# The input sums of a Winograd MLP spread over a chunk's third and fourth double pair, and the first row of a spectrum made one item for both batches

## The chip, the core and the metric

The kernel runs on one core of a Trainium2 chip. The core has five engines with an instruction queue each: TensorE (PE, with its weight loads shown apart as PEld), VectorE (DVE), ScalarE (ACT), GpSimd (POOL) and SyncE (SP), which here issues nearly all DMAs. An engine takes its instructions in order; between engines they wait for each other through semaphores. The metric is the device time of one execution in microseconds, lower is better.

## What is computed

Three stages follow each other on x of shape (2, 3008, 256), all in float32: a real FFT along the sequence with a complex linear layer, a soft threshold of 0.01 and the inverse FFT; a SiLU MLP (256 to 2048 to 256); a leaky-ReLU MLP of the same size.

```python
X = np.fft.rfft(x, axis=1)
Yr = Xr @ w_r - Xi @ w_i + b_r
Yi = Xr @ w_i + Xi @ w_r + b_i
Yr = np.sign(Yr) * np.maximum(np.abs(Yr) - lam, 0.0)
...
y = np.fft.irfft(Y, n=x.shape[1], axis=1)
...
h = x @ w_in
g = h * (1.0 / (1.0 + np.exp(-h)))
return (g @ w_out).astype(np.float32)
...
g = np.maximum(0.01 * h, h)
```

## The kernel before

Every float32 product is made of three matmuls: each operand is split into a high part (`hi`, a cast) and a low part (`lo`, the operand minus `hi`), and lo x hi, hi x lo and hi x hi are added up in PSUM.

The order of instructions is written out by hand (`manual_schedule`): the program's order is each engine's order.

**The spectrum.** 3008 is 47 x 64. A first DFT over 47 (`pa`, line 284) leaves rows k = 0 to 23 for each of two batches. An *item* (k, b) is one row of one batch; the list `items` has 48. The function `spectrum(j)` runs a pipeline over items: `mix` (matmuls `pz`, the complex linear layer), `split_z` (cast `zh`, subtraction `zl`), `seed` (the bias is copied into the PSUM tile `py`), `forward` (six `py` matmuls with the table `dm` of that k), `threshold`, `split_y`, `backward` (three `pb` matmuls), `store` (a DMA to a buffer `scr` in DRAM). `load_dm` and `split_dm` bring and split the tables ahead of time. Row k = 0 is real and has one column for each batch: `mix` runs once for both, then item (0, 0) uses rows 0 to 63 of the result and of the table and item (0, 1) uses rows 64 to 127, each with its own `forward` on 64 rows, `backward` and `store`.

Between the items, `fifth_w` runs a fifth of a step of the decoding of the first MLP's weights: the raw tile `wraw` is loaded by SyncE and made into `wc` and `wm` by ScalarE first (lines 142 and 144). The tiles `pz` have two buffers in PSUM.

**The inverse** (`inverse`, line 444) reads `scr` back as `bt`, 96 rows of which two are zero.

**The MLPs** work through 12 chunks of 512 tokens (the last of 384) in each layer, and in each chunk through eight pairs of 128 hidden units. In chunks 2 to 10 of the second layer (`FAST`) pairs go two at a time, as a *double pair*; `both_pairs` writes out the order of one, and a chunk has four, with p = 0, 2, 4 and 6. In it `pr` is the even pair, whose first layer is made plainly (`first`), and `fa` the odd pair, whose first layer is made with Winograd's seven products (`unit`, line 619): products 1 and 2, later 6 and 7, then 5 and 4, then 3. Product 7 begins anew in the PSUM tile that product 2 had filled, so it waits until `join` on VectorE (line 627, `f<-ph,kept`) has read it; `join` also reads the copy `kept` that ScalarE makes. `one` and `two` are the pairs of the double pair before, whose second layer (`products`, line 690) is made here. For `one`, VectorE's first operation in a double pair is `low("1")` (`l<-f,h`).

Products 5, 6 and 7 and 4 read sums of the chunk's input blocks, which are made one chunk ahead. `ahead` gives the steps of this as a list: load the input (`load_x2`), split it (`split_x2`), make four sums (`sums_x2`: t1 and t3 on GpSimd, then t2 and t4 on VectorE, where t2 reads t1), split the sums (`split_xs`: two casts on ScalarE, one subtraction on VectorE, one on GpSimd). `make_next` takes one step from the list: in the middle of a double pair (after `pr.low("1")`), but at its end (after `fa.t1()`) where p is 4. So a chunk's four double pairs hold load, split, sums, split of the sums, one each. For chunk 2 the steps stand in the ordinary pairs of chunk 1.

Of the kernel before, what the change touches and what calls it, by code (L numbers as in the profile page):

```python
# [9 lines left out]
F32 = mybir.dt.float32  # L10
# [3 lines left out]
ALU = mybir.AluOpType  # L14
# [25 lines left out]
def dft_tables():  # L40
# [13 lines left out]
    for k in range(KH):  # L54
# [16 lines left out]
        dm[k, 0, :, 4], dm[k, 1, :, 4] = wt * s, wt * sg * c  # L71
    dm[0, 1, :, :3] = dm[0, 0, :, :3]

    dm[..., 3:, :] = dm[..., 3:, :].reshape(KH, 2, R2, 2, R2 // 2, 2).swapaxes(-1, -2).reshape(KH, 2, R2, 2, R2)
    as32 = lambda a, *sh: np.ascontiguousarray(a.reshape(sh).astype(np.float32))
    da = np.concatenate([da[:80], np.zeros((NP - NM, 128)), da[80:]])
    return as32(da, NP, 128), as32(ea, NJ, PAIR), as32(dm, KH, 128, 320)


@with_exitstack  # L80
def spectral_mlp_kernel(ctx, tc, x, w_r, w_i, b_r, b_i, w_in1, w_out1, w_in2, w_out2, da, ea, dm, out):
# [13 lines left out]

    scr = dram.tile([KH * 4, B, R2 // 2, D], F32, name="scr")
    scr2 = dram.tile([128, 2, TOK], F32, name="scr2")
    ea_sb = const.tile([NJ, PAIR], F32, name="ea_sb")

# [127 lines left out]
    bias = fft.tile([128, D], F32, name="bias")  # L227
    items = [(k, b) for k in range(KT) for b in range(B)] + [(k, b) for b in range(B) for k in range(KT, KH)]
    dm_raw, dm_t, z_p, z_t, y_p, y_t, b_p = ({} for _ in range(7))

    def new_dm(j):
        return j < len(items) and (items[j][0] >= KT or items[j][1] == 0)

    def load_dm(j):
# [17 lines left out]
    with tc.tile_pool(name="xp", bufs=6) as xp:  # L252
# [27 lines left out]
        for c in range(R2 // NA):  # L280
# [19 lines left out]
            if c == 10:  # L300
                for g, w in enumerate((w_r, w_i)):
                    nc.sync.dma_start(out=wms[g], in_=w.rearrange("(h p) e -> p h e", p=128))
            elif c == 11:
                load_dm(0)
                for g, w in enumerate((b_r, b_i)):
                    nc.sync.dma_start(out=bias[g * 64:(g + 1) * 64, :], in_=w.rearrange("(o e) -> o e", o=1).to_broadcast([64, D]))
                load_dm(2)
            elif c == 12:
                nc.sync.dma_start(out=ea_sb, in_=ea)
            elif c == 13:  # L310
                for g in range(2):
                    nc.scalar.copy(wm["hi"][:, :, g], wms[g])
                    nc.gpsimd.tensor_tensor(out=wm["lo"][:, :, g], in0=wms[g], in1=wm["hi"][:, :, g].bitcast(F32), op=ALU.subtract)
# [7 lines left out]
    def mix(j):  # L321
        k, b = items[j]
        if j == 1:
            return
        r = B * (B * (k - 1) + b + 1) if k else 0
# [10 lines left out]
    def split_z(j):  # L336
        if j == 1:
            z_t[1] = z_t[0]
            return
        pz = z_p.pop(j)  # L340
        hi = f3.tile([128, 2, D], F32R, tag="zh", name="zh")
        lo = f3.tile([128, 2, D], F32R, tag="zl", name="zl")
        src = pz.rearrange("p (g e) -> p g e", g=2)
        nc.scalar.copy(hi, src)
        nc.vector.tensor_tensor(out=lo, in0=src, in1=hi.bitcast(F32), op=ALU.subtract)
        z_t[j] = hi, lo

    def seed(j):
        if j in y_p:
            return  # L350
        y_p[j] = ps_h.tile([128, 512], F32, tag="h", name="py")[:, :D]
# [63 lines left out]
    seed(1)  # L415
    spectrum(-1)
    n_items = len(items)
    for j in range(n_items):
# [53 lines left out]

    def sums_x2(c):
        b = [quarter(x2f[c][h], k) for h in range(2) for k in range(2)]
        t = xsum[c] = [stage.tile([128, 512], F32, tag="wraw", name="xsum", bufs=2) for _ in range(2)]
        t1, t2, t3, t4 = (quarter(u, k) for u in t for k in range(2))
        for d, x, y, eng in ((t1, b[1], b[0], nc.gpsimd), (t3, b[3], b[1], nc.gpsimd),
                             (t2, b[3], t1, nc.vector), (t4, b[2], t2, nc.vector)):
            eng.tensor_tensor(out=d, in0=x, in1=y, op=ALU.subtract)  # L479
        xs[c] = homes[c % 2].tile([128, 2, 1024], F32R, tag="hold0", name="xs")  # L480

# [299 lines left out]
    def both_pairs(i):  # L781
# [170 lines left out]
```

## Time and profile before

| | |
|---|---|
| median of 3 runs | 1161.02 us (1160.89 to 1161.34) |
| the profiled execution | 1160.99 us, span 1159.0 us |
| TensorE busy | 1141.4 us, 98% of the span |
| VectorE busy | 867.5 us, 75% |
| ScalarE busy | 816.7 us, 70% |
| GpSimd busy | 668.5 us, 58% |
| granted TensorE clock | 1.0 throughout |

The span runs from the first to the last instruction; 2 us of the execution's time lie outside it. A matmul's end is modelled, so what a matmul costs in a dense stretch is read from the distance of the starts. The chain that ended last runs over TensorE for 82% of the span. The list `todo` is what moves work between engines in the second layer, and the waits there are read in one double pair of one chunk and hold for the others.

### The profile page before, as it was taken

The page shows a single profiled execution, that of the slowest core. Times are in us where ns is not written, and L with a number is a line of the kernel's source. Part 1 is how long each engine was busy: PE and PEld are TensorE (multiplying, and loading weights), DVE is VectorE, ACT ScalarE, POOL GpSimd, SP SyncE. Part 2 cuts the span into 40 slices and gives each one's busy share as a digit, 9 for nine tenths or more (in the row PEclk, how much of TensorE's full clock was granted, in tenths as well). Part 3 has the DMA queues.
Part 4 walks back from the last instruction along what each step waited for, and adds up shares of the span by engine and source line. Part 5 has one row for each costly group of instructions (what it writes and reads, how often), then busy time and mean ns, then how long its engine had stood idle before and what let it go on. Part 6 is the DMA issues. An engine that isn't in the chain of part 4 may idle for free.

```text
span 1159.0 us, 21096 instructions
## 1 busy us (share of the span) xinstructions
PE 1141.4 (98%) x7608; PEld 1052.2 (91%) x7608; DVE 867.5 (75%) x1484; ACT 816.7 (70%) x1720; POOL 668.5 (58%) x683
## 2 busy tenths in 40 slices
PE   9999999999999999999999999999999999999998
PEld 9888888889999999999999999989899889988998
DVE  4898956455666666676674778899999999999973
ACT  4788876666676676666666777777777777777774
POOL 0567836444444444454453777767677677667652
PEclk9999999999999999999999999999999999999999
DMA  9445543010111210111110111010000100101000
GB/s 243 120 135 158 167 120 93 20 51 19 57 54 38 68 60 29 51 60 35 38 37 1 37 32 37 20 37 20 26 30 20 37 20 20 37 20 33 20 6 27
DMA packets 36184, 61.80 MB, mean 53 GB/s; under 512 B 3952, under 2 KB 16080, under 8 KB 36080
## 3 DMA queue, kind: packets, MB, share of 16 engines
q1 hardware_dynamic: 35792, 60.28, 17.4%
q8 instruction: 60, 0.98, 0.4%
q14 instruction: 44, 0.36, 0.1%
q10 hardware_dynamic: 288, 0.18, 0.1%
HBM read 41.83 MB, written 18.61 MB: 52 GB/s over the span
## 4 chain that ended last, share of the span: by engine, by line
PE 82%; DVE 9%; issue 4%; POOL 2%; ACT 2%; DMA 0%; SPq 0%; ACTq 0%; POOLq 0%
PE acc L690 33%; PE ph L582 31%; PE pz L332 6%; PE ph L619 4%; PE py L361 3%; PE px L444 2%; PE pa L284 2%; DVE u L664 2%; DVE l L645 2%; PE pb L384 1%; DVE f L627 1%; POOL u L657 1%; DVE lb L645 1%; POOL la L645 1%; DVE xsum L479 1%
## 5 line engine op out<-in xcount | busy, mean ns | idle before, releaser
L645 POOL TENSOR_TENSOR la<-u,ha 128x512 fp32r<-128x512 f32 (+1 forms) x176 | 245.4, 1395 | 199.7 <-ACT ha L683 195.2
L645 DVE TENSOR_TENSOR lb<-u,hb 128x768 fp32r<-128x768 f32 (+1 forms) x176 | 193.7, 1100 | 154.6 <-ACT hb L683 154.0
L582 PE MATMUL ph<-xhi,winhi 128*128 128x512 f32 (+1 forms) x624 | 188.1, 382 | 0.0
L582 PE MATMUL ph<-xlo,winhi 128*128 128x512 f32 (+1 forms) x624 | 188.0, 381 | 0.0
L582 PE MATMUL ph<-xhi,winlo 128*128 128x512 f32 (+1 forms) x624 | 187.2, 380 | 0.1
L657 POOL TENSOR_TENSOR u<-u 128x256 f32<-128x256 f32 x160 | 150.9, 943 | 32.0 <-ACT u L597 22.2
L683 ACT CAST hb<-u 128x768 fp32r<-128x768 f32 (+1 forms) x176 | 141.2, 802 | 33.5 <-DVE u L671 31.5
L690 PE MATMUL acc<-hb,wlo 128*128 128x256 f32 (+1 forms) x496 | 137.8, 278 | 0.0
L690 PE MATMUL acc<-lb,whi 128*128 128x256 f32 (+1 forms) x496 | 137.5, 277 | 0.0
L690 PE MATMUL acc<-hb,whi 128*128 128x256 f32 (+1 forms) x496 | 137.5, 277 | 0.0
L582 PEld LDWEIGHTS ph<-xhi,winhi 128*128 128x128 f32 x624 | 116.4, 187 | 21.7
L582 PEld LDWEIGHTS ph<-xlo,winhi 128*128 128x128 f32 x624 | 116.4, 187 | 21.3 <-POOL xlo L467 0.3
L582 PEld LDWEIGHTS ph<-xhi,winlo 128*128 128x128 f32 x624 | 104.4, 187 | 9.6 <-ACT u L599 0.2
L683 ACT CAST ha<-u 128x512 fp32r<-128x512 f32 (+1 forms) x176 | 109.1, 620 | 3.6 <-PE acc L690 1.9
L597 ACT ACTIVATE ph<-ph 128x512 f32<-128x512 f32 (+1 forms) x112 | 64.7, 578 | 63.8 <-PE ph L582 63.8
L690 PE MATMUL acc<-ha,wlo 128*128 128x256 f32 (+1 forms) x352 | 99.1, 282 | 0.0
L690 PE MATMUL acc<-ha,whi 128*128 128x256 f32 (+1 forms) x352 | 98.8, 281 | 0.0
L690 PE MATMUL acc<-la,whi 128*128 128x256 f32 (+1 forms) x352 | 98.8, 281 | 0.0
L690 PE MATMUL acc<-h,wlo 128*128 128x256 f32 (+1 forms) x336 | 94.7, 282 | 0.0
L597 ACT ACTIVATE u<-ph 128x512 f32<-128x512 f32 (+1 forms) x80 | 47.1, 588 | 67.1 <-PE ph L582 65.2
L690 PE MATMUL acc<-l,whi 128*128 128x256 f32 (+1 forms) x336 | 93.6, 278 | 0.0
L690 PE MATMUL acc<-h,whi 128*128 128x256 f32 (+1 forms) x336 | 93.5, 278 | 0.0
(157 smaller groups left out, 3099.8 us busy)
## 6 DMA issues: line engine op xcount, KB each, us to landing
wraw<-in_moe_w_in_dram SPq DMA_DIRECT2D x32, 256.0 KB
wraw<-in_moe_w_out_dram SPq DMA_DIRECT2D x32, 256.0 KB
scr<-bo SPq DMA_DIRECT2D x48, 128.0 KB
scr<-x2o SPq DMA_DIRECT2D x22, 256.0 KB
x2i<-scr SPq DMA_DIRECT2D x22, 256.0 KB
out_dram<-x2o SPq DMA_DIRECT2D x22, 256.0 KB
dmr<-in_dm_dram SPq DMA_DIRECT2D x34, 160.0 KB
bt<-scr SPq DMA_DIRECT2D x14, 384.0 KB
```

Of the source, the lines that this page charges most:

```text
L284: nc.tensor.matmul(pa[h][:, s * 128:(s + 1) * 128], lhsT=xt[c][:, s, h * 128:(h + 1) * 128], rhs=da_sb, start=True, stop=True, skip_group_ ...
L332: nc.tensor.matmul(turned(pz), lhsT=u[:, h, :], rhs=turned(v[:, h].rearrange("p g e -> p (g e)")), start=(n == 0), stop=(n == len(terms) - 1))
L361: nc.tensor.matmul(turned(py), lhsT=u, rhs=turned(v), start=False, stop=(n == len(terms) - 1), skip_group_check=True)
L444: nc.tensor.matmul(px[:, s * PAIR:(s + 1) * PAIR], lhsT=bt[:, s, h * 128:(h + 1) * 128], rhs=ea_sb, start=True, stop=True, skip_group_chec ...
L582: nc.tensor.matmul(turned(ph), lhsT=u[:, h, f % HALF * 128:][:, :128], rhs=turned(v[:, h, :]), start=(i == 0), stop=(i == len(terms) - 1))
L597: nc.scalar.activation(out=out, in_=ph, func=ACTF.Silu)
L619: nc.tensor.matmul(turned(self.ph[dst]), lhsT=u, rhs=turned(m), start=(begin and i == 0), stop=(i == 2), skip_group_check=True)
L645: eng.tensor_tensor(out=lo, in0=src, in1=hi.bitcast(F32), op=ALU.subtract)
L657: nc.gpsimd.tensor_tensor(out=blk(1), in0=blk(0), in1=blk(2), op=ALU.subtract)
L664: nc.vector.tensor_tensor(out=v[:, 3:5], in0=b22, in1=v[:, 0:2], op=ALU.subtract)
L683: nc.scalar.copy(hi, src)
L690: nc.tensor.matmul(turned(dst), lhsT=u, rhs=turned(v), start=(begin and self.p == 0 and i == 0), stop=(end and self.p == NF // 2 - 1 and i ...
```

## The change

There are two parts.

*The sums.* `sums_x2` is split in two steps: the first makes t1 and t3 on GpSimd, the second t2 and t4 on VectorE. `make_next` is called in the middle of the fourth double pair as before and now also at its end (`pr.p >= 4`). So the four double pairs hold load; split; GpSimd's sums (at the end); VectorE's sums (in the middle) and the split of the sums (at the end).

*Row k = 0.* The items become 47: (0, 0) stands for both batches. Its table is built anew so that one `forward` on 128 rows makes the real and imaginary parts of both batches; it needs a second table (`dm[KH]`, 128 of its columns, called "rest" here) for the second matmul of each kind, which is loaded and split ahead (`load_rest`, `split_rest`). Its bias tile `bias0` (printed as `bias_103` or `bias0_103`) is filled by two broadcasts, and two single rows of it are then written again with `b_r`. It is stored by two DMAs of half the size. Two zero rows go from `scr`, `ea` and `bt` (94 for 96).

```diff
-    dm[0, 1, :, :3] = dm[0, 0, :, :3]
-
...
+    dm = np.concatenate([dm.reshape(KH, 128, 320), np.zeros((1, 128, 320))])
+    dm[0] = 0
...
+        u0, u1, back = dm[0, :, 64:192], dm[KH, :, :128], dm[0, :, 192:]
+        u0[n, q], u1[n, q] = c[:, :-1], s[:, :-1]
...
-    items = [(k, b) for k in range(KT) for b in range(B)] + [(k, b) for b in range(B) for k in range(KT, KH)]
+    bias0 = fft.tile([128, D], F32, name="bias0")
+    items = [(0, 0)] + [(k, b) for k in range(1, KT) for b in range(B)] + [(k, b) for b in range(B) for k in range(KT, KH)]
...
+    def split_rest():
+        hi, lo = (dmp.tile([128, 320], F32R, tag=q, name=q, bufs=7)[:, :128] for q in ("dmh", "dml"))
+        raw = dm_raw.pop("rest")[:, :128]
+        nc.scalar.copy(hi, raw)
+        nc.gpsimd.tensor_tensor(out=lo, in0=raw, in1=hi.bitcast(F32), op=ALU.subtract)
+        dm_t["rest"] = hi, lo
...
-                load_dm(2)
+                load_rest()
+                load_dm(1)
+                for r0, r1, w in ((0, 64, b_r), (64, 128, b_i)):
+                    nc.sync.dma_start(out=bias0[r0:r1, :], in_=w.rearrange("(o e) -> o e", o=1).to_broadcast([64, D]))
+                for r0 in (64, 96):
+                    nc.sync.dma_start(out=bias0[r0:r0 + 1, :], in_=b_r.rearrange("(o e) -> o e", o=1))
...
-        if j == 1:
-            return
...
-        nc.vector.tensor_copy(y_p[j], bias)
+        nc.vector.tensor_copy(y_p[j], bias if j else bias0)
...
-        rows = slice(j * 64, j * 64 + 64) if j < 2 else slice(0, 128)
-        terms = [(u[rows, 64 * (1 - g):64 * (3 - g)], v[rows, g, :]) for u, v in ((dl, zh), (dh, zl), (dh, zh)) for g in range(2)]
+        tables = [[u[:, 64 * (1 - g):64 * (3 - g)] for g in range(2)] for u in (dh, dl)]
+        if j == 0:
+            for t, u in zip(tables, dm_t.pop("rest")):
+                t[1] = u
+        dh, dl = tables
+        terms = [(u[g], v[:, g, :]) for u, v in ((dl, zh), (dh, zl), (dh, zh)) for g in range(2)]
...
-        nc.sync.dma_start(out=scr[4 * k:4 * k + 4, b], in_=bo)
+        if k:
+            nc.sync.dma_start(out=scr[4 * k - 2:4 * k + 2, b], in_=bo)
+        else:
+            for b in range(B):
+                nc.sync.dma_start(out=scr[0:2, b], in_=bo[b * R2:(b + 1) * R2, :])
...
+    split_rest()
...
-        fifth_w(j % 5 if j < 2 * KT else (j - 2 * KT) % 3)
+        fifth_w(j % 5 if j < 2 * KT - 1 else (j - 2 * KT + 1) % 3)
...
-    def sums_x2(c):
+    def sums_x2(c, late_ones):
...
+        for d, x, y in ((t2, b[3], t1), (t4, b[2], t2)) if late_ones else ((t1, b[1], b[0]), (t3, b[3], b[1])):
+            (nc.vector if late_ones else nc.gpsimd).tensor_tensor(out=d, in0=x, in1=y, op=ALU.subtract)
...
-                    lambda: sums_x2(c), lambda: [split_xs(c, k, e) for k, e in engines]]
+                    lambda: sums_x2(c, False), lambda: sums_x2(c, True), lambda: [split_xs(c, k, e) for k, e in engines]]
...
-        if pr.p == 4:
+        if pr.p >= 4:
```

On VectorE, before, from the end of a third double pair to the first `join` of the next chunk (the first and last `lb` here end a double pair):

```order
L645 TENSOR_TENSOR lb<-u,hb 128x768
L479 TENSOR_TENSOR xsum<-x2i,xsum 128x256 x2
L645 TENSOR_TENSOR l_9682<-f_9602,h_9681 128x512
L627 TENSOR_TENSOR f_9735<-ph,kept 128x256
...
L645 TENSOR_TENSOR lb<-u,hb 128x768
L645 TENSOR_TENSOR l_9730<-ph,h_9729 128x512
L485 TENSOR_TENSOR xs<-xsum,xs 128x512
L645 TENSOR_TENSOR lb<-u,hb 128x768
L645 TENSOR_TENSOR l_9819<-f_9735,h_9818 128x512
L627 TENSOR_TENSOR f_9865<-ph,kept 128x256
```

The same engine in the change, from the first `join` of the fourth double pair to the first `join` of the next chunk:

```order
L663 TENSOR_TENSOR f_9723<-ph,kept 128x256
...
L681 TENSOR_TENSOR lb<-u,hb 128x768
L681 TENSOR_TENSOR l_9718<-ph,h_9717 128x512
L516 TENSOR_TENSOR xsum<-x2i,xsum 128x256 x2
L681 TENSOR_TENSOR lb<-u,hb 128x768
L521 TENSOR_TENSOR xs<-xsum,xs 128x512
L681 TENSOR_TENSOR l_9805<-f_9723,h_9804 128x512
L663 TENSOR_TENSOR f_9855<-ph,kept 128x256
```

The sums moved from ahead of the fourth double pair's first `join` to behind its `l<-ph,h`, and `xs` moved from there to behind the second `lb`; three operations instead of one stand between that `l` and the next chunk's first `join`.

On SyncE in the change, at the start of the spectrum, with the semaphores that each DMA waits for (`dmr_347` is the rest table, `dmr_349` the table of k = 1, lanes DMAHW0 to 7 count landings):

```order
L337 DMA bias0_103<-in_b_r_dram 64x256 [waits DMAHW2_49]
L337 DMA bias0_103<-in_b_i_dram 64x256 [waits DMAHW3_49]
L339 DMA bias0_103<-in_b_r_dram 1x256 [waits DMAHW4_49,DMAHW3_49]
L339 DMA bias0_103<-in_b_r_dram 1x256 [waits DMAHW5_49]
L341 DMA ea_sb_76<-in_ea_dram 94x94 [waits DMAHW6_49]
L150 DMA wraw_402<-in_moe_w_in_dram 128x512 [waits DMAHW7_49]
```

The four DMAs of `bias0` are new and stand ahead of `ea_sb` and the first `wraw`; the third waits on the lane of the second (DMAHW3).

On ScalarE in the change, at the same place:

```order
L273 CAST dmh<-dmr 128x320
L257 CAST dmh<-dmr 128x128
L157 ACTIVATE wc<-wraw 128x256
L159 ACTIVATE wm<-wraw 128x256
L371 CAST zh<-pz 128x512 x2
```

The cast of the rest table is new; `wc` and `wm` of the first `wraw` stand ahead of the first `zh`, as before.

## Rows read from the trace of the kernel before

**Rows 1.** The page, part 1: engine, busy us (share), instructions.

```profile
PE 1141.4 (98%) x7608; PEld 1052.2 (91%) x7608; DVE 867.5 (75%) x1484; ACT 816.7 (70%) x1720; POOL 668.5 (58%) x683
```

**Rows 2.** Waits of TensorE: waiter, releaser, us in total, times, longest.

```profile
PE ph L619 <- DVE f L627: 12.7, 8, 1.6
```

**Rows 3.** Timeline of TensorE: start, length, line, out<-in, count, idle before; chunk 5.

```profile
871.50 0.85 PE L619 MATMUL ph<-xs,ws 128*128 128x256 f32 x6
...
901.48 0.50 PE L619 MATMUL ph<-xs,ws 128*128 128x256 f32 x3
903.57 0.63 PE L619 MATMUL ph<-xs,ws 128*128 128x256 f32 x3 [1.58 <-DVE f L627]
```

**Rows 4.** Timeline of VectorE, third to fourth double pair of chunk 5 and on.

```profile
899.68 1.81 DVE L479 TENSOR_TENSOR xsum<-x2i,xsum 128x256 f32<-128x256 f32 x2 [1.33 <-POOL xsum L479]
901.42 1.75 DVE L645 TENSOR_TENSOR l<-f,h 128x512 fp32r<-128x512 f32 x1
...
908.16 1.18 DVE L485 TENSOR_TENSOR xs<-xsum,xs 128x512 fp32r<-128x512 f32 x1
909.26 2.04 DVE L645 TENSOR_TENSOR lb<-u,hb 128x768 fp32r<-128x768 f32 x1
```

**Rows 5.** Timeline of VectorE, first double pair of chunk 5.

```profile
869.41 1.22 DVE L645 TENSOR_TENSOR l<-f,h 128x512 fp32r<-128x512 f32 x1
870.56 0.41 DVE L627 TENSOR_TENSOR f<-ph,kept 128x256 f32<-128x256 f32 x1
...
875.72 0.68 DVE L645 TENSOR_TENSOR l<-ph,h 128x512 fp32r<-128x512 f32 x1
876.33 1.45 DVE L645 TENSOR_TENSOR lb<-u,hb 128x768 fp32r<-128x768 f32 x1
```

**Rows 6.** Timeline of GpSimd, first and fourth double pair of chunk 5.

```profile
875.57 1.39 POOL L645 TENSOR_TENSOR la<-u,ha 128x512 fp32r<-128x512 f32 x1 [2.63 <-ACT ha L683]
...
898.91 1.44 POOL L479 TENSOR_TENSOR xsum<-x2i 128x256 f32<-128x256 f32 x2
...
901.18 1.45 POOL L645 TENSOR_TENSOR la<-u,ha 128x512 fp32r<-128x512 f32 x1
```

**Rows 7.** Timeline of ScalarE, fourth double pair of chunk 5.

```profile
900.17 0.36 ACT L624 COPY kept<-ph 128x256 f32<-128x256 f32 x1
```

**Rows 8.** Timeline of TensorE, start of the spectrum and one later period.

```profile
36.57 0.61 PE L332 MATMUL pz<-wmhi,ahi 128*128 128x512 f32 x2
...
40.97 0.38 PE L332 MATMUL pz<-wmhi,alo 128*128 128x512 f32 x1
...
97.44 0.62 PE L332 MATMUL pz<-wmlo,ahi 128*128 128x512 f32 x2
...
98.80 0.39 PE L361 MATMUL py<-zh,dml 128*128 128x256 f32 x2
...
99.82 0.62 PE L332 MATMUL pz<-wmlo,ahi 128*128 128x512 f32 x2
```

**Rows 9.** Timeline of SyncE's DMA issues, start of the spectrum.

```profile
26.00 0.58 SPq L306 DMA_DIRECT2D bias<-in_b_r_dram  x1
27.15 0.49 SPq L306 DMA_DIRECT2D bias<-in_b_i_dram  x1
...
28.94 1.88 SPq L135 DMA_DIRECT2D wraw<-in_moe_w_in_dram  x2
...
35.42 0.33 SPq L237 DMA_DIRECT2D dmr<-in_dm_dram  x1
```

**Rows 10.** Timelines of ScalarE and VectorE, start of the spectrum.

```profile
34.33 0.45 ACT L142 ACTIVATE wc<-wraw 128x256 uint32<-128x256 uint32 x1
...
35.88 0.58 ACT L344 CAST zh<-pz 128x512 fp32r<-128x512 f32 x1 [0.74 <-PE pz L332]
...
36.50 0.69 DVE L345 TENSOR_TENSOR zl<-pz,zh 128x512 fp32r<-128x512 f32 x1 [0.54 <-ACT zh L344]
```

**Rows 11.** Windows: stretch, length, busy us (instructions), clock, DMA share, GB/s.

```profile
36.00:37.30 1.30, 1.30 (x7) 0.85 (x6) 0.80 (x2) 0.54 (x2) 0.75 (x1) 1.00 0.47 126
```

More of the change, by code (lines that the diff above doesn't have):

```diff
@@ L71, in dft_tables @@
         dm[k, 0, :, 4], dm[k, 1, :, 4] = wt * s, wt * sg * c
-    dm[0, 1, :, :3] = dm[0, 0, :, :3]
     dm[..., 3:, :] = dm[..., 3:, :].reshape(KH, 2, R2, 2, R2 // 2, 2).swapaxes(-1, -2).reshape(KH, 2, R2, 2, R2)
+    dm = np.concatenate([dm.reshape(KH, 128, 320), np.zeros((1, 128, 320))])
+    dm[0] = 0
+    th = 2 * np.pi * ((R1 * np.arange(R2 // 2 + 1)[:, None] * n2[None, :]) % S) / S
+    c, s = np.cos(th).T, np.sin(th).T
+    s[:, -1] = 0
+    half = R2 // 2
+    for b in range(B):
+        n, q = slice(b * R2, (b + 1) * R2), slice(b * half, (b + 1) * half)
+        im = slice(R2 + b * half, R2 + (b + 1) * half)
+        u0, u1, back = dm[0, :, 64:192], dm[KH, :, :128], dm[0, :, 192:]
+        u0[n, q], u1[n, q] = c[:, :-1], s[:, :-1]
+        u0[n, im], u1[n, im] = -s[:, :-1], c[:, :-1]
+        u0[n, im.start], u1[n, im.start] = c[:, -1], s[:, -1]
+        order = lambda a: a.reshape(-1, half, 2).swapaxes(-1, -2).reshape(-1, R2)
+        back[q, n] = order(c[:, :-1].T * np.where(np.arange(half) == 0, 1.0, 2.0)[:, None] / S)
+        back[im, n] = order(-2 * s[:, :-1].T / S)
+        back[im.start, n] = order(c[:, -1:].T / S)[0]
     as32 = lambda a, *sh: np.ascontiguousarray(a.reshape(sh).astype(np.float32))
     da = np.concatenate([da[:80], np.zeros((NP - NM, 128)), da[80:]])
-    return as32(da, NP, 128), as32(ea, NJ, PAIR), as32(dm, KH, 128, 320)
+    return as32(da, NP, 128), as32(np.delete(ea.reshape(NJ, PAIR), (2, 3), 0), NR, PAIR), as32(dm, KH + 1, 128, 320)
 @with_exitstack
@@ L94, in spectral_mlp_kernel @@
     stage = pool("stage", 3)
-    scr = dram.tile([KH * 4, B, R2 // 2, D], F32, name="scr")
+    scr = dram.tile([NR, B, R2 // 2, D], F32, name="scr")
     scr2 = dram.tile([128, 2, TOK], F32, name="scr2")
-    ea_sb = const.tile([NJ, PAIR], F32, name="ea_sb")
+    ea_sb = const.tile([NR, PAIR], F32, name="ea_sb")
     parts = ("hi", "lo")
@@ L232, in new_dm, with load_rest @@
         return j < len(items) and (items[j][0] >= KT or items[j][1] == 0)
+    def load_rest():
+        dm_raw["rest"] = dmp.tile([128, 320], F32, tag="dmr", name="dmr", bufs=3)
+        nc.sync.dma_start(out=dm_raw["rest"], in_=dm[KH])
+    def split_rest():
[4 more added lines that the diff above has]
+        dm_t["rest"] = hi, lo
     def load_dm(j):
@@ L336, in split_z @@
     def split_z(j):
-        if j == 1:
-            z_t[1] = z_t[0]
-            return
         pz = z_p.pop(j)
@@ L390, in store @@
         nc.scalar.copy(bo, b_p.pop(j))
-        nc.sync.dma_start(out=scr[4 * k:4 * k + 4, b], in_=bo)
+        if k:
+            nc.sync.dma_start(out=scr[4 * k - 2:4 * k + 2, b], in_=bo)
+        else:
+            for b in range(B):
+                nc.sync.dma_start(out=scr[0:2, b], in_=bo[b * R2:(b + 1) * R2, :])
     STAGES = [(split_z, 1), (threshold, 3), (split_y, 4), (seed, 1), (store, 6), (mix, 0), (forward, 2), (backward, 5)]
@@ L409, in load_b @@
             b, p = divmod(g, R2 // 2)
-            bt = btp.tile([NJ, NG, D], F32, tag="bt", name="bt")
+            bt = btp.tile([NR, NG, D], F32, tag="bt", name="bt")
             nc.sync.dma_start(out=bt[:, :n], in_=scr[:, b, p:p + n, :])
@@ L471, in spectral_mlp_kernel @@
     quarter = lambda a, k: a[:, k * 256:(k + 1) * 256]
-    def sums_x2(c):
+    def sums_x2(c, late_ones):
         b = [quarter(x2f[c][h], k) for h in range(2) for k in range(2)]
[L475 to L480, printed above, removed]
+        if not late_ones:
+            xsum[c] = [stage.tile([128, 512], F32, tag="wraw", name="xsum", bufs=2) for _ in range(2)]
+            xs[c] = homes[c % 2].tile([128, 2, 1024], F32R, tag="hold0", name="xs")
+        t1, t2, t3, t4 = (quarter(u, k) for u in xsum[c] for k in range(2))
+        for d, x, y in ((t2, b[3], t1), (t4, b[2], t2)) if late_ones else ((t1, b[1], b[0]), (t3, b[3], b[1])):
+            (nc.vector if late_ones else nc.gpsimd).tensor_tensor(out=d, in0=x, in1=y, op=ALU.subtract)
     def split_xs(c, k, eng):
```

## The prediction, made before the change was timed

> **What bounds the kernel now.** The page was read first, then the waits of TensorE, then the stretches where it waits, engine by engine. TensorE (PE) is busy for 98% of the span [rows 1], so a change can win only by removing its matmuls or its waits. The waits view names one wait of weight: the matmuls of `unit` (line 619) stand 8 times, 1.6 us at the longest, for VectorE's `join` (line 627) [rows 2]. Its other lines are small and lie at the start of the program.
>
> Rows 3 show one of the eight, in chunk 5 of the second MLP layer. The three matmuls of product 6 start at 901.48; a 256-column matmul takes a slot of 0.114 us (1.02 for nine [rows 8]), so product 7 is due at 901.82, and it starts at 903.57. The true cost is thus 1.75 us (the view counts 1.58, from the modelled end of the matmul before). In the chunk's first double pair the same six matmuls run without a gap [rows 3]: product 7 is there at 871.50 + 0.35 = 871.85. Eight waits (chunks 2 to 9, which prepare chunks 3 to 10) cost 8 x 1.75 = 14.0 us.
>
> Why VectorE is late [rows 4]: it stands from 898.35 for 1.33 us in front of its two input sums (`xsum`), since their first operand comes from GpSimd, whose own two `xsum` start at 898.91 [rows 6]. The sums take 1.81, then `l<-f,h` takes 1.75 (it runs beside GpSimd's `la`, 901.18 to 902.63 [rows 6]), and `join` comes behind it; product 7 starts when it is done. ScalarE is not the cause: its `kept` copy, the other input of `join`, ends at 900.53 [rows 7].
>
> **Part 1, the sums and their splits.** GpSimd's two sums stay at the end of the third double pair. VectorE's two go to the middle of the fourth, ahead of its second `lb`; the split of the sums (two ScalarE casts, one subtraction on VectorE, one on GpSimd) goes from there to the end of the fourth. Nothing is added: one chunk has the same instructions.
>
> Gain at the old place: VectorE's `l<-f,h` can follow `lb` at about 898.6, and `join` then waits only for `kept`, as it does in the first double pair (870.56, just behind `l<-f,h` [rows 5]). So `join` ends near 901.0, before 901.82, and the 1.75 us are gone there.
>
> What is late next is the same queue one double pair on. The fourth double pair now runs as the first does, 901.82 - 871.85 = 29.97, call it 30.0 us later. VectorE's `l<-ph,h` ended at 876.40 there [rows 5], so it ends at 906.40 here. Behind it stand the two sums, `lb`, the split `xs`, `l<-f,h` and the next chunk's first `join`; product 7 of that chunk is due one double pair (10.0 us) after 901.82, at 911.8. The pieces, each from its nearest row: the sums 0.82 (two 256-column operations at the 0.41 of a `join` [rows 5]) to 1.81 [rows 4]; `lb` 1.45 [rows 5] to 2.04 [rows 4]; `xs` 1.18 [rows 4] to 1.75, the longest 512-column operation [rows 4]; `l<-f,h` 1.22 [rows 5] to 1.75 [rows 4]; `join` 0.41. Five starts overlap the end before them by 0.08 each (876.33 against 876.40), 0.4 in all.
> Low ends: 0.82 + 1.45 + 1.18 + 1.22 + 0.41 - 0.4 = 4.7, so 911.1: no wait. High ends: 1.81 + 2.04 + 1.75 + 1.75 + 0.41 - 0.4 = 7.4, so 913.8: a wait of 2.0.
> Taken: sums 1.81, since GpSimd's `la` of the fourth double pair stands beside them until about 906.96 (875.57 + 1.39 + 30.0 [rows 6]) and its `u` next; `lb` 1.65, between its ends, since GpSimd's half of the split can start only behind the second ScalarE cast; `xs` 1.18, `l<-f,h` 1.22. Sum 5.9, so 912.3: a new wait of 0.5 us at the next chunk's first double pair. Each chunk gains 1.75 - 0.5 = 1.25, eight gain **10.0 us** (bounds: 14.0 gained to 2.0 lost).
>
> VectorE operations with one operand in PSUM (`l<-ph,h`) show 0.68 beside `la`; those with two operands in SBUF stretch: `l<-f,h`, which begins 0.24 after `la`, ends at 903.17, that is 0.54 after `la` [rows 4, 6]. The Trainium skill (SBUF — State Buffer, "Who interferes with whom") says that a VectorE instruction with two SBUF inputs and a GpSimd instruction that reads SBUF exclude each other, the second one blocked until the first is over; the row agrees. By that rule every moved operation could be held for a whole GpSimd instruction, which is the second rival below.
>
> Who else sees the moved work: ScalarE's two casts now precede the cast `h<-f` that `l<-f,h` reads. The second cast waits for the second sum (908.1 by the terms above); two casts behind that, at about 0.6 each as `zh` [rows 10], end near 909.4, and `l<-f,h` is reached only at 910.7. So ScalarE costs nothing here as long as VectorE's queue covers it; without that cover `join` would come up to 0.6 earlier than ScalarE allows, inside the bounds. TensorE reads the split sums first in products 6 and 7, so these come no later than `join` itself. No DMA moves.
>
> The first preparation (for chunk 2) lies in ordinary pairs; its split moves from the seventh to the eighth pair, right ahead of chunk 2's first `join`. No row prices it; its bounds are nothing and one `xs` (1.18). Taken: **0.5 us lost**, once.
>
> **Part 2, row k = 0 as one item.** Batch 1's item goes: six `py` and three `pb` matmuls of 256 columns. In a steady period these take 99.82 - 98.80 = 1.02 us and the six `pz` matmuls 98.80 - 97.44 = 1.36 [rows 8], on the path, since TensorE bounds this stage too: **1.02 gained**. The two k = 0 items were also the only matmuls on 64 rows. From 36.57 to 40.97 [rows 8] TensorE did five pairs of `pz` matmuls (five thirds of 1.36, or 2.27) and two `py` groups (two thirds of 1.02 each, or 1.36): 3.63 of 4.40 us, so about 0.76 are gaps. **0.76 gained** if they go with the 64-row matmuls.
> The Trainium skill (TensorEngine Tiling (Array Packing), "Key Properties") says that a change of tiling mode drains TensorE. By it all of the 0.76 goes; the rows alone only place the gaps between the two kinds of matmul, and would leave the gain of this item anywhere between nothing and all of it.
>
> What it adds, at the start: one table load in place of a later one, two more broadcasts for `bias0`, and two single-row DMAs that overwrite part of the second broadcast, so SyncE waits for that to land before it issues them (the order after shows the wait). `ea_sb` and the first `wraw` loads are queued behind them. ScalarE needs the first `wraw` for `wc` and `wm`, which stand ahead of the first `zh` in its order. Before, `wraw` was issued at 28.94 [rows 9] and had long landed when `wc` ran at 34.33 [rows 10]. After: the two `bias` broadcasts took 1.64 (26.00 to 27.64 [rows 9]); with the rest table, table 1 and `bias0` the second broadcast is issued at about 30.2. A table load that met an idle queue was issued at 35.42 [rows 9] and moved its bytes between 36.0 and 37.3 [rows 11], so a landing comes at least 1.9 after the issue: 32.1, or 33.0 behind the backlog. Then two rows, `ea_sb` and `wraw` at 0.4 each: `wraw` issued at 33.3 to 34.2, landed 1.9 to 3.0 later, at 35.2 to 37.2. From `wc` to the end of the first `zl` it takes 0.45 twice (`wc`, and `wm` of the same size), 0.58 and 0.69, less the overlaps about 2.1 [rows 10], and the third `pz` group needs the buffer that this `zl` frees. TensorE is ready for it at 37.05. With `wraw` at 36.5, TensorE waits until 38.7: **1.7 lost**; bounds 0.3 and 2.3.
> The rest (one item fewer per engine, 94 for 96 rows in the inverse, one weight step fewer in the loop) lies beside TensorE, which shows no wait from there to the second layer [rows 2]. Part 2 sums to -1.02 - 0.76 + 1.7, about **0.1 gained**.
>
> **The sum.** Against the profiled execution (1160.99, 0.03 from the median of the runs): 1160.99 - 10.0 + 0.5 - 0.1 = **1151.4 us**.
>
> **The rivals.** (1) The wait does not come back: the low ends hold, each chunk gains 1.75: 1160.99 - 14.0 + 0.3 - 0.1 = 1147.2. For it: the sums no longer start right behind two GpSimd instructions. Against: three operations instead of one stand in the next `join`'s queue. (2) GpSimd gets in first and holds most of that queue: sums 1.81, `lb` 2.04, `xs` 1.18, `l<-f,h` 1.75, `join` 0.41 give 913.2, a new wait of 1.4, and 1160.99 - 8 x 0.35 + 0.9 - 0.1 = 1159.0. For it: `lb` already takes 2.04 where the split stands beside it [rows 4]. Against: GpSimd's half of the split waits for ScalarE's second cast, which needs the second sum. (3) Slower: all of the queue is held at the high ends, a wait of 2.0 at the next first double pair, more than the 1.75 removed. It decides from 1.75 on; with 1.2 for chunk 2 and 0.6 lost at the start it gives 1160.99 + 2.0 + 1.2 + 0.6 = 1164.8.
>
> **How the numbers follow.** The forecast (a new wait of 0.2 to 1.0) has 0.55, rival 1 0.22, rival 2 (1.0 to 1.75) 0.17, rival 3 0.06. The range cuts a tenth on each side: below, the wait all but gone, 1146.5; above, a wait of about 1.3, 1157.5. A measurement of this kernel can tell about 0.2% (2.3 us) from no change. Faster by more than that: the first two cases and 0.10 of rival 2, 0.87; within: 0.07; slower: 0.06.
>
> **What would show it.** Right: no wait of `unit` in fourth double pairs; a short one (0.2 to 1.0) in the first double pairs of chunks 3 to 10, on `join`; each of these chunks about 1.2 shorter; the first `zh` 1 to 2 us later than 35.88, behind `wc`; no gaps at the first `py` groups. Wrong: waits above 1 us at the first double pairs, any wait elsewhere in the chunk, or a first `zh` that is not late.

## The result, and the profile after

The changed kernel takes **1177.13 us** (median; runs from 1175.80 to 1177.51) against 1160.97 before: a ratio of 1.0137, interval 1.0119 to 1.0154. It is slower by 16 us, where 1151.4 was forecast and 1157.5 was the end of the range. The profiled execution took 1175.8 with a span of 1174.0. One execution among those of the experiments below took 1625.24 us at a granted clock of 0.66, and no figure here uses it.

Page, part 1 (engine, busy us and share, instructions; before: [rows 1]):

```profile
PE 1152.8 (98%) x7599; PEld 1060.3 (90%) x7599; DVE 864.9 (74%) x1482; ACT 815.9 (70%) x1718; POOL 664.5 (57%) x683
```

TensorE runs nine matmuls fewer in this page, as the change says, and is busy 11.4 us longer. Matmuls that become slower without becoming more point at the clock, and the waits of TensorE (waiter, releaser, us in total, times, longest) say where to look:

```profile
PE acc L726 <- ACT ha L686: 7.5, 3, 3.1
PE ph L655 <- DVE f L663: 3.7, 8, 0.5
PE px L480 <- issue: 3.2, 1, 3.2
PE pz L362 <- DVE zl L372: 1.8, 1, 1.8
```

The eight waits of 1.6 [rows 2] have become eight of about 0.5, as forecast. Three lines of weight are new: the wait at the start, forecast at 1.7, and two that no step of the prediction held, 10.7 us in four waits. Windows of the changed kernel (stretch, length, then busy us and instructions of PE, PEld, DVE, ACT, POOL, then granted clock, DMA share, GB/s) place them:

```profile
34.00:50.00 16.00, 14.20 (x70) 11.68 (x69) 10.48 (x24) 9.46 (x23) 7.47 (x11) 0.89 0.36 110
...
100.00:150.00 50.00, 47.79 (x301) 42.76 (x299) 44.13 (x93) 40.97 (x109) 39.97 (x54) 1.00 0.49 149
150.00:250.00 100.00, 91.16 (x414) 76.03 (x415) 45.49 (x104) 56.87 (x141) 43.36 (x61) 0.92 0.22 73
```

Between 100 and 250 us TensorE stands for 11 us, and from 150 on its clock is 0.92 on average. In the kernel before the same two windows have a TensorE that never stands, at a clock of 1.00:

```profile
100.00:150.00 50.00, 50.00 (x328) 45.41 (x328) 44.17 (x95) 41.68 (x113) 37.35 (x50) 1.00 0.54 163
150.00:250.00 100.00, 100.00 (x472) 83.68 (x471) 53.62 (x123) 67.74 (x166) 52.42 (x76) 1.00 0.22 67
```

So the loss lies where the inverse begins to read the spectrum back, not in the fast chunks.

What is different there is the read-back of the spectrum (`bt<-scr`, 94 rows where there were 96). Narrow windows around it, first of the changed kernel, then of the kernel before:

```profile
143.00:146.00 3.00, 3.00 (x20) 2.64 (x19) 2.30 (x6) 2.86 (x9) 2.31 (x4) 1.00 0.13 50
148.00:150.00 2.00, 0.00 (x0) 0.00 (x0) 0.00 (x0) 0.00 (x0) 0.00 (x0) 0.97 0.15 57
150.00:156.00 6.00, 5.03 (x23) 5.06 (x24) 1.34 (x3) 1.77 (x5) 0.00 (x0) 0.50 0.33 111
```

```profile
137.50:138.50 1.00, 1.00 (x9) 0.92 (x9) 0.97 (x2) 0.86 (x3) 1.00 (x2) 1.00 0.70 243
139.50:140.50 1.00, 1.00 (x11) 1.00 (x10) 1.00 (x3) 0.79 (x2) 0.84 (x2) 1.00 0.94 328
```

While the 96 rows are read back, 0.70 to 0.94 of the 16 DMA engines' time is busy, at up to 328 GB/s (a few other DMAs included). With 94 rows it is 0.13, about what 2 of 16 would give (0.125), at 50 GB/s; from 148 to 150 no engine computes anything. SyncE's DMA issues (start, length, line, out<-in, count) and three pieces of the chain of waits show what stands behind it:

```profile
141.03 0.74 SPq L446 DMA_DIRECT2D bt<-scr  x2
141.82 7.17 SPq L423 DMA_DIRECT2D scr<-bo  x2
149.04 2.45 SPq L150 DMA_DIRECT2D wraw<-in_moe_w_in_dram  x1
```

```profile
156.33 0.28 ACT bo L421
156.63 11.43 DMA scr<-bo
168.09 0.37 ACT bo L421
...
172.16 7.94 DMA wraw<-in_moe_w_out_dram
...
195.83 9.92 DMA wraw<-in_moe_w_out_dram
```

A store of `bo` needs 11.4 us to land; ScalarE stands in its order at the next `bo`, and with it `wc`, `wm` and `ha`; weight loads need 7.9 and 9.9. In the kernel before ScalarE waits for no DMA between 130 and 215 us. The four waits of TensorE (of `px` at 150.97, of `acc` at 172.56, 184.29 and 207.50) cost 11.3 us by the spacing of the starts. Behind each of them the matmuls run at half rate for a while: the window 150 to 156 shows a clock of 0.50, the lower of the two levels (1.2 of 2.4 GHz), and 0.92 over 100 us is some 8 us of work lost. Together that is some 19 of the 20.0 us by which the changed kernel falls back between 147.6 us (2.5 behind the same matmuls before) and 212 us (22.4 behind).

### The profile page after: what moved, and what is told of

Its sections match the earlier page's. It is cut to its first block, busy times and chain, and to the rows that moved or that the text cites. A ratio compares the mean times of both kernels' runs of the same rounds, so it can differ in the third digit from the quotient of the medians.

```text
span 1174.0 us, 21067 instructions
## 1 busy us (share of the span) xinstructions
PE 1152.8 (98%) x7599; PEld 1060.3 (90%) x7599; DVE 864.9 (74%) x1482; ACT 815.9 (70%) x1718; POOL 664.5 (57%) x683
## 4 chain that ended last, share of the span: by engine, by line
PE 87%; DVE 6%; DMA 3%; issue 1%; ACT 1%; POOL 0%; SPq 0%; DVEq 0%; ACTq 0%; POOLq 0%
PE acc L726 36%; PE ph L618 32%; PE ph L655 7%; PE pz L362 5%; PE py L392 2%; PE px L480 2%; PE pa L311 2%; DMA wraw<-in_moe_w_out_dram 2%; DVE l L681 1%; DVE xsum L516 1%; PE pb L415 1%; DMA scr<-bo 1%; DVE xs L521 1%; DVE f L663 1%; DVE lb L681 1%
## 5 line engine op out<-in xcount | busy, mean ns | idle before, releaser
L681 DVE TENSOR_TENSOR lb<-u,hb 128x768 fp32r<-128x768 f32 (+1 forms) x176 | 186.3, 1058 | 155.4 <-ACT hb L719 154.9
```

The source lines that it names most:

```text
L681: eng.tensor_tensor(out=lo, in0=src, in1=hi.bitcast(F32), op=ALU.subtract)
```

## The experiments

The first four kernels shared the runs of the kernel before (1160.95), and so did the next four (1161.36); the last two had their own (1160.73 and 1161.58).

**The 94 rows alone**, on the kernel before, with both items of k = 0 as they were; rows 2 and 3, the imaginary half of k = 0, which the inverse needs nothing of, are neither stored nor read:

```diff
-    return as32(da, NP, 128), as32(ea, NJ, PAIR), as32(dm, KH, 128, 320)
+    return as32(da, NP, 128), as32(np.delete(ea.reshape(NJ, PAIR), (2, 3), 0), NR, PAIR), as32(dm, KH, 128, 320)
...
-        nc.sync.dma_start(out=scr[4 * k:4 * k + 4, b], in_=bo)
+        if k:
+            nc.sync.dma_start(out=scr[4 * k - 2:4 * k + 2, b], in_=bo)
+        else:
+            nc.sync.dma_start(out=scr[0:2, b], in_=bo[:R2, :])
...
-            bt = btp.tile([NJ, NG, D], F32, tag="bt", name="bt")
+            bt = btp.tile([NR, NG, D], F32, tag="bt", name="bt")
```

> The kernel before with one thing of the change alone: the buffer, its read-back and the inverse table have 94 rows for 96; items, sums and everything else are as before. Theory A (a read-back of 94 rows moves on two of the 16 DMA engines: DMA share 0.12 to 0.13 there in the changed kernel, where 96 rows showed 0.7 to 0.9; stores and weight tiles queue behind it): about 20 us slower than before, 1177 to 1184, with the waits at the first inverse and in the first MLP chunks and the low clock behind them. Theory B (the loss comes from the merged item: one weight step fewer, one item fewer to hide the loads): within 1 us of before, 1160 to 1162.

Measured: 1182.19 (1181.51 to 1182.92), ratio 1.0184 (1.0169 to 1.0199): 21.2 us lost, with no merged item and no moved sums. Its waits of TensorE:

```profile
PE acc L693 <- ACT ha L653: 7.7, 3, 3.1
PE px L447 <- DMA bt<-scr: 3.6, 1, 3.6
```

The same two waits in nearly the same sizes. Two rows fewer in the array cost more than the whole change loses.

**The change with 96 rows**: the two spare rows hold a second copy of row k = 0 and meet zeros in the table.

```diff
-    scr = dram.tile([NR, B, R2 // 2, D], F32, name="scr")
+    scr = dram.tile([NJ, B, R2 // 2, D], F32, name="scr")
...
-                nc.sync.dma_start(out=scr[0:2, b], in_=bo[b * R2:(b + 1) * R2, :])
+                for r in (0, NR):
+                    nc.sync.dma_start(out=scr[r:r + 2, b], in_=bo[b * R2:(b + 1) * R2, :])
...
-            bt = btp.tile([NR, NG, D], F32, tag="bt", name="bt")
+            bt = btp.tile([NJ, NG, D], F32, tag="bt", name="bt")
```

> The changed kernel with 96 rows in the buffer, its read-back and the inverse table again (the last two rows are a second copy of the row k = 0, against zeros in the table); all else as changed. Theory A: the 20 us between the first inverse and 211 us are gone, the start (about 2.5 lost) and the sums (7.7 gained) stay: 1154 to 1158. Theory B: 1175 to 1178, as the changed kernel.

Measured: 1155.38 (1153.64 to 1156.76), ratio 0.9952 (0.9937 to 0.9967). 21.75 us of the change are gone by this edit alone. Its waits of TensorE, and the window of the start:

```profile
PE ph L656 <- DVE f L664: 3.9, 8, 0.5
PE pz L362 <- DVE zl L372: 2.0, 1, 2.0
```

```profile
34.00:50.00 16.00, 14.00 (x68) 11.64 (x68) 10.35 (x26) 9.46 (x24) 6.89 (x10) 0.89 0.35 110
```

The waits at `px` and `acc` are gone; the start still has its wait of 2.0, and behind it a clock of 0.89 over 16 us, 1.8 us of work.

**The sums alone**, on the kernel before (the diff's part in `sums_x2`, in the list of steps and in `both_pairs`, and nothing else).

> The kernel before with the sums' part alone. From the two traces, the second layer's double-pair stretch is 7.7 us shorter in the changed kernel: 1152.5 to 1154.5 if the parts don't touch each other. Rival: part of the 7.7 came from what the first part shifted (where the loads of the second layer fall), then 1155 to 1158.

Measured: 1154.06 (1153.61 to 1154.35), ratio 0.9940 (0.9923 to 0.9957). This part gains 6.9 us, and without the other it would have been the better change. TensorE's line for `join` is 4.3 us in nine waits.

**94 rows in two loads of 80 and 14.**

```diff
-            nc.sync.dma_start(out=bt[:, :n], in_=scr[:, b, p:p + n, :])
+            for r0, r1 in ((0, 80), (80, NR)):
+                nc.sync.dma_start(out=bt[r0:r1, :n], in_=scr[r0:r1, b, p:p + n, :])
```

> The changed kernel with each 94-row read-back made by two DMAs, of 80 and of 14 rows. Theory A, that the number of rows in one DMA decides on how many engines it moves: the 80 rows move on all 16, so 1154 to 1160. Rival, that 94 rows cost as such (the matmuls on 94 rows, the odd size in the buffer): 1173 to 1178. Theory B: 1175 to 1178.

Measured: 1155.63 (1153.79 to 1157.65), ratio 0.9955 (0.9940 to 0.9970): the same as with 96 rows. The window of the read-back:

```profile
141.00:144.00 3.00, 3.00 (x22) 2.74 (x21) 2.96 (x8) 2.40 (x6) 2.83 (x5) 1.00 0.81 233
```

The same bytes from the same array at a DMA share of 0.81: not 94 rows as such cost the time, but 94 rows in one load. The Trainium skill (DMA: Bandwidth & Descriptors, "Why a DMA increments its semaphore by 16 and not by 1") states the rule: a DMA runs on the largest number of engines, at most 16, that divides the slowest dimension of both sides. By it 94 gives 2 engines, 96 and 80 give 16, 14 gives 14; the shares of 0.13, 0.94 and 0.81 agree.

**The start: broadcasts that do not overlap**, on the change with 96 rows.

```diff
-                for r0, r1, w in ((0, 64, b_r), (64, 128, b_i)):
-                    nc.sync.dma_start(out=bias0[r0:r1, :], in_=w.rearrange("(o e) -> o e", o=1).to_broadcast([64, D]))
-                for r0 in (64, 96):
-                    nc.sync.dma_start(out=bias0[r0:r0 + 1, :], in_=b_r.rearrange("(o e) -> o e", o=1))
+                for r0, r1, w in ((0, 65, b_r), (65, 96, b_i), (96, 97, b_r), (97, 128, b_i)):
+                    nc.sync.dma_start(out=bias0[r0:r1, :], in_=w.rearrange("(o e) -> o e", o=1).to_broadcast([r1 - r0, D]))
```

> The changed kernel with 96 rows (1155.38), and the bias of the merged item loaded as four broadcasts of rows that do not overlap (0 to 64, 65 to 95, 96, 97 to 127), so that none of SyncE's four issues waits for another to land. Theory A (the wait of TensorE of 2.0 at the third group of pz comes from the two single-row loads, which hold SyncE and with it the first weight load; and the granted clock of 0.89 between 34 and 50 us, 1.8 us of work, follows from that wait): both go, 1155.38 - 3.8 = 1151.6, between 1150.5 and 1152.5, and the window 34 to 50 shows a clock of 1.00. Rival B (it is the larger number of loads ahead of the weights in SyncE's queue, the extra table of 160 KB and the second bias): the weights still land late, a wait of at least 1 us stays at pz, 1154 or more. Rival C (the clock falls there for another reason): the wait goes, the clock stays at 0.89, 1153.4.

Measured: 1153.61 (1153.48 to 1157.45), ratio 0.9943 (0.9925 to 0.9961). The profiled execution waits 0.6 at `pz` and keeps a clock of 1.00. That lies between theory A and rival B and fits neither range: the first weight load is issued at 32.59, still 3.65 later than before [rows 9].

**The merged item alone**, in that form, with the sums as before.

> The kernel before with the merged item alone (96 rows, bias in four broadcasts that do not overlap), sums as before. Theory A (the item itself is worth what the prediction put on it: 1.02 us of matmuls and 0.76 us of gaps): 1160.95 - 1.8 = 1159.2, between 1158 and 1160. Rival B (it saves no time even without a wait at the start, since the start is bounded by weight loads): 1161 to 1162. By the difference of the runs with and without the item so far (1155.38 with its wait, 1154.06 without it) the item with its wait costs 1.3 us.

Measured: 1160.98 (1159.34 to 1164.33), ratio 0.9998 (0.9989 to 1.0007). On the median nothing is gained, but its ten runs fall into two groups: five from 1159.34 to 1160.04, inside theory A's range, and five from 1161.91 to 1164.33. The profiled execution (1161.91) is one of the second group. Rows of its start (waits of TensorE; timeline of ScalarE; the window) and one row of a later period (timeline of TensorE):

```profile
PE pz L360 <- DVE zl L370: 2.1, 1, 2.1
```

```profile
37.34 0.43 ACT L157 ACTIVATE wc<-wraw 128x256 uint32<-128x256 uint32 x1 [2.67 <-DMA wraw<-in_moe_w_in_dram]
```

```profile
34.00:50.00 16.00, 13.87 (x78) 11.64 (x77) 12.48 (x28) 10.64 (x27) 7.64 (x12) 1.00 0.35 108
```

```profile
98.03 0.62 PE L360 MATMUL pz<-wmlo,ahi 128*128 128x512 f32 x2
```

The weight loads went out at 32.47, and here TensorE waited 2.1 again, where the same start in the run before, with the loads at 32.59, waited 0.6: `wc` could begin 4.9 us after the issue here and 3.3 there (35.86). So the start varies from run to run with the landing of the weights, and the late issue leaves no room for it; the two single rows are not the whole cause. Whether the pieces of 65 and 31 rows that this form loads are slow themselves was not tested. The item's own gain does show in this trace: TensorE begins the spectrum 0.04 later than in the kernel before and loses 2.3 at the wait by the starts, and at 98.03 it is 0.59 behind the same group of the kernel before (97.44 [rows 8]), so some 1.7 are gained, and they stay to the end of the spectrum. With that, rival B (no time saved even without a wait) is not shown.

**The sums in another order**, on the kernel before: load in the middle of a chunk's first double pair, input splits in the middle of the second, GpSimd's sums at its end, VectorE's sums in the middle of the third, their splits in the middle of the fourth. Against the sums alone:

```diff
-        if pr.p != 4:
-            make_next()
+        make_next()
         two.products("b")
...
-        if pr.p >= 4:
+        if pr.p == 2:
             make_next()
```

> The sums part alone on the kernel before, in another order of steps: load in the middle of a chunk's first double pair, splits of the input in the middle of the second, GpSimd's sums at the end of the second, VectorE's sums in the middle of the third, splits of the sums in the middle of the fourth; nothing is left at the end of the fourth. With the change's order alone the kernel takes 1154.06, and TensorE still waits 4.3 us in nine waits for join 0 of the next chunk's first double pair, with some 0.15 us behind each. Theory A (those waits come only from the splits of the sums at the end of the fourth double pair, which take VectorE away ahead of the next join): no wait of TensorE for a join above 0.2 us is left, 1154.06 - 4.3 - 1.3 = 1148.5, between 1147 and 1149.5. Rival B (VectorE has no room in the middle of the third double pair either, where its sums of 1.8 us now stand): waits of 0.5 or more come back in the third or fourth double pair, 1152 to 1155. Rival C (GpSimd, now with sums at the end of the second double pair, holds VectorE up by the port that they share): the waits stand in the third double pair's first half, 1151 to 1154.

Measured: **1147.60** (1147.25 to 1147.81), ratio 0.9880 (0.9866 to 0.9895), faster than both kernels. All waits of TensorE that its view lists:

```profile
PE warm L272 <- DVE idle L269: 1.2, 1, 1.2
PE pa L284 <- DMA xt<-in_x_dram: 0.2, 1, 0.2
```

No wait for `join` is left in any chunk. Theory A holds; the 13.4 to 13.8 us gained are the 14.0 that the prediction put on the eight old waits.

**Both last edits together.**

> The merged item with 96 rows and with the bias in four broadcasts that do not overlap, and the sums in the other order (load, splits, GpSimd's sums in the first two double pairs, VectorE's sums in the middle of the third, splits of the sums in the middle of the fourth): the last two edits together. Theory A (the start and the fast chunks do not touch each other, so the two gains add up): 1151.6 - 5.6 = 1146.0, between 1144.5 and 1148. Rival B (either of the two edits brings no gain): about 1149 to 1152. Rival C (neither does): 1154 to 1156.

Measured: runs of 1146.23, 1147.68 and 1151.87, ratio 0.9889 (0.9866 to 0.9912), a profiled wait of 0.7 at `pz` (1147.68). That is not distinguishable from the sums in the other order without the item. Two runs lie in theory A's range and one at the end of rival B's, so this decides nothing.

**The item's extra loads on ScalarE's queue**, added to that. They were meant to go out at about 15 us; in ScalarE's order their turn came at 21.67 to 23.64.

> The sums in the order of e6_sums_spread (1147.6) and the merged item with 96 rows, its extra loads (the second table of 160 KB and the four broadcasts of its bias) issued by ScalarE in the middle of the first stage (around 15 us) and no longer by SyncE at 28 to 32 us. In the runs so far the first weight load was issued at 28.9 before, at 33.9 in the change's form and at 32.5 with four broadcasts, and TensorE waited 0, 2.0 and 0.6 to 2.1 us for the splits of z behind it. Theory A (what costs the item its gain is only the place of its extra loads ahead of the weights on SyncE): weights issued at about 29 again, no wait at pz above 0.2, and the item's 1.8 us show: 1147.6 - 1.8 = 1145.8, between 1145 and 1146.8. Theory B (the DMA engines are full in the first 34 us, share 0.95, and 288 KB more delay everything behind them at about 240 GB/s, 1.2 us): the input or the weights land later, 1146.8 to 1148. Theory C (ScalarE's five issues hold up its copies of pa, and TensorE with them): waits at pa in the first stage, 1147.5 to 1150.

Measured: 1152.85 (1151.38 to 1153.60), ratio 0.9928 (0.9915 to 0.9942): slower by 5.3 us than the sums alone in that order, and outside all three ranges. Timeline of TensorE, windows, and a wait of SyncE between 8 and 42 us:

```profile
29.91 10.63 PE L311 MATMUL pa<-da_sb,xt 96*128 96x128 f32 x64 [2.83 <-DMA xt<-in_x_dram]
```

```profile
0.00:34.00 34.00, 29.95 (x219) 29.03 (x220) 12.61 (x27) 12.40 (x28) 0.20 (x4) 0.94 0.82 215
34.00:50.00 16.00, 15.92 (x96) 14.02 (x96) 10.77 (x24) 9.60 (x23) 8.48 (x11) 0.91 0.43 131
```

```profile
SPq L288 <- DMA dmr<-in_dm_dram: 3.6, 1, 3.6
```

The input came late by 2.8 us, and the clock was at 0.94 and 0.91 in the two windows, another 3.5 us of work. Theory B's reason does not fit: from 16 to 24 us the DMA share was 0.53 to 0.66, where the kernel before has 1.04, so the engines were not full. SyncE's next input load stood until 23.9 for the landing of the second table, which ScalarE had issued at 21.67, and the first weight load was issued at 34.18, not at 29, so theory A was not put to the test.

**The item with its bias made in place**: VectorE copies the loaded bias into the item's tile and two single rows of it over rows 64 and 96, and only the 128 columns of the second table that are used are loaded.

```diff
-        nc.vector.tensor_copy(y_p[j], bias if j else bias0)
+        nc.vector.tensor_copy(y_p[j], bias)
+        if j == 0:
+            for r in (64, 96):
+                nc.vector.tensor_copy(y_p[0][r:r + 1, :], bias[r - 64:r - 63, :])
```

> The sums in the order of e6_sums_spread (1147.6) and the merged item with 96 rows, without a second bias in memory: VectorE copies the bias that is loaded anyway into the item's tile and two single rows of it over rows 64 and 96; of the second table only the 128 columns that are read are loaded. Ahead of the weights SyncE then has one more load (64 KB) than before, where the change has five more and e7_both six. Theory A (the loads ahead of the weights cost the item its gain): the first weight load is issued at 29 to 30 us, no wait at pz above 0.3, and the item's 1.8 us show in part or whole: 1145.5 to 1147. Theory B (VectorE's two more copies of some 0.4 us before the first splits of z delay these): a wait of 0.5 to 1 at pz, 1147 to 1148. Theory C (the item is worth nothing at the start whatever is loaded): 1147.5 to 1149 with no wait at pz.

Measured: 1147.22 (1147.02 to 1147.76), ratio 0.9877 (0.9861 to 0.9894): the fastest, by less than can be told from 1147.60. Its timeline of TensorE shows where the item's gain goes in this execution, beside that of the sums in the other order (second fence), which lacks the item and begins the spectrum within 0.2 us of it. The third fence has ScalarE and VectorE at its start:

```profile
39.31 0.39 PE L390 MATMUL py<-zh,dml 128*128 128x256 f32 x2
...
40.00 0.62 PE L357 MATMUL pz<-wmlo,ahi 128*128 128x512 f32 x2
...
56.02 0.62 PE L357 MATMUL pz<-wmlo,ahi 128*128 128x512 f32 x2
...
61.53 0.71 PE L357 MATMUL pz<-wmlo,ahi 128*128 128x512 f32 x2 [0.16 <-DVE zl L367]
```

```profile
56.99 0.62 PE L332 MATMUL pz<-wmlo,ahi 128*128 128x512 f32 x2
...
61.76 0.62 PE L332 MATMUL pz<-wmlo,ahi 128*128 128x512 f32 x2
```

```profile
36.09 0.59 ACT L366 CAST zh<-pz 128x512 fp32r<-128x512 f32 x1 [0.54 <-PE pz L357]
...
36.80 0.43 DVE L374 COPY py<-bias 128x256 f32<-128x256 f32 x1
37.14 0.68 DVE L367 TENSOR_TENSOR zl<-pz,zh 128x512 fp32r<-128x512 f32 x1
```

The first weight load was issued at 30.35, and `wc` did not wait for it. (Both last edits together have five more loads ahead of the weights than before, as the change has, not six.) Yet TensorE waited 0.46 at the third `pz` group: `zh` ended at 36.68, and `zl` came only at 37.14, behind VectorE's copies of the bias. That is theory B, and the time lies in its range. The same group of `pz` starts 0.97 earlier than without the item at 56.02, and 0.23 earlier at 61.53; from 66 us on 0.1 is left. In this execution the lead goes in short waits for VectorE's `zl`. Why VectorE and ScalarE are just late enough there was not followed further; in the traces of the item alone and of both last edits together what the item gained up to 50 us is kept to the end of the spectrum. So theory C (the item is worth nothing whatever is loaded) is not shown.

## Why the prediction was wrong, step by step

**The step that failed** is the last sentence on part 2: "The rest (one item fewer per engine, 94 for 96 rows in the inverse, one weight step fewer in the loop) lies beside TensorE". For the 94 rows the cover was TensorE's lack of waits before [rows 2], and that was taken without asking how long the read-back lasts or what is queued behind it. It cost 21.2 us alone and 21.75 within the change. A DMA with another row count is a changed operation, the trace of before held no load of 94 rows that could price it, and so it needed bounds like every other unknown cost; the Trainium skill's rule on engines per DMA, cited at the run with 80 and 14 rows, would have given 2 engines for 16. No rival contained it, so the range missed too; with 96 rows the change takes 1155.38, inside the range.

**The sums.** The mechanism was right. The waits left the fourth double pairs, and new ones came where forecast, at the first double pairs of chunks 3 to 10. Timelines of chunk 5's first double pair after, TensorE, then VectorE, then GpSimd (start, length, line, operation):

```profile
890.32 0.51 PE L655 MATMUL ph<-xs,ws 128*128 128x256 f32 x3
891.08 0.62 PE L655 MATMUL ph<-xs,ws 128*128 128x256 f32 x3 [0.25 <-DVE f L663]
```

```profile
885.18 1.80 DVE L516 TENSOR_TENSOR xsum<-x2i,xsum 128x256 f32<-128x256 f32 x2
886.90 0.95 DVE L681 TENSOR_TENSOR lb<-u,hb 128x768 fp32r<-128x768 f32 x1
887.77 1.78 DVE L521 TENSOR_TENSOR xs<-xsum,xs 128x512 fp32r<-128x512 f32 x1
889.47 1.22 DVE L681 TENSOR_TENSOR l<-f,h 128x512 fp32r<-128x512 f32 x1
890.61 0.41 DVE L663 TENSOR_TENSOR f<-ph,kept 128x256 f32<-128x256 f32 x1
```

```profile
887.71 1.29 POOL L521 TENSOR_TENSOR xs<-xsum,xs 128x512 fp32r<-128x512 f32 x1 [1.02 <-ACT xs L520]
```

The queue from the first sum to the end of `join` takes 5.84 (885.18 to 891.02) where 5.9 was summed, though two pieces are off in opposite ways: `lb` 0.95 for 1.65, and `xs` 1.78 for 1.18, beside GpSimd's own half of the split; that the sum comes out so close is luck. In this chunk product 7 starts 0.76 behind product 6, whose three slots of 0.114 take 0.34: 0.42 are lost. In most of the others the same difference is 1.0, so 0.65 are lost; the waits view, which counts from modelled ends, gives 3.7 for the eight. Forecast was 0.5 each. The term was too large all the same: 10.0 forecast, 7.7 measured between chunk 2 and chunk 10 within the change, 6.9 by the sums alone. Part of the rest are short waits in the double pairs that follow, which the sum held at nothing. Chunk 2's loss of 0.5 did not come: its product 7 has 1.14 of room, as in the kernel of the sums alone.

**The start.** The wait came at the third `pz` group as described, in the timeline of SyncE and of TensorE:

```profile
30.90 0.60 SPq L337 DMA_DIRECT2D bias<-in_b_i_dram  x1
33.62 0.59 SPq L339 DMA_DIRECT2D bias<-in_b_r_dram  x2
...
34.55 0.83 SPq L150 DMA_DIRECT2D wraw<-in_moe_w_in_dram  x2
```

```profile
39.57 0.71 PE L362 MATMUL pz<-wmlo,ahi 128*128 128x512 f32 x2 [1.80 <-DVE zl L372]
```

It is 1.96 by the starts for 1.7 forecast (weights issued at 34.55, for 33.3 to 34.2). Not forecast was the clock behind it, 0.89 in the window 34 to 50, another 1.8. The 0.76 of gaps did go: in the run with the bias in place the first `py` group takes 0.69 from 39.31 to 40.00, where six full slots of 0.114 are 0.68. The Trainium skill's rule on tiling modes, named in the prediction, agrees with that. So the gain of 1.8 was about right in size; what was mis-sized is what it is set against. The item came with a wait of 0.5 to 2.8 for the first splits in every form that kept its loads on SyncE, partly with a lower clock behind it, and in one trace its lead went in later waits. On the medians no form with the item is faster than the same kernel without it by more than can be told.

**The sum again with what was measured**: 1160.97 - 6.9 (sums) + 1.3 (the item at the start: 1155.38 against 1154.06) + 21.75 (94 rows) = 1177.1, and 1177.13 was measured. These terms are differences along a chain of runs that ends at the change, so they must add up to it. A check is the price of the 94 rows measured alone, 21.2: it gives 1176.6.

## What to carry to other kernels

When an array loses a row or two, price the transfer of the new shape, not only the arithmetic; keep row counts that split over all DMA engines, with rows of zeros if need be. Work that takes VectorE away costs nothing while every chain through it keeps some room, so spread preparation over a chunk instead of moving it from one crowded end to the next. A load put ahead of others in a queue is paid by whatever is behind it, here the first weights; moved to ScalarE's queue it held up SyncE's input loads instead.

## What the runs showed of the hardware that was not expected

While loads of 94 rows were under way the DMA engines moved 50 GB/s at a share of 0.13, and with loads of 96 rows, or of 80 and 14, 233 to 328 GB/s at 0.70 to 0.94 in the windows shown. Unrelated stores and weight loads behind it landed after 7.9 to 11.4 us.

A wait of TensorE can cost about twice its length, since matmuls behind it may run at the lower clock level: the waits of 11.3 us were followed by some 8 us of lost work, the start's 1.8 to 2.0 by 1.8. It does not always happen: behind 2.0 us the clock of the window 34 to 50 was 0.89 in the change with 96 rows, and behind 2.1 us it was 1.00 in the item alone; the eight waits of up to 1.6 us of the kernel before [rows 2] left it at 1.00. What decides it is left open.
